# Decay rows fetched by one transfer per pair and sub-block, running products stored block by block, decays read back by one transfer per block

## The chip, the cores and the metric

The kernel runs on one core of a Trainium2 chip. The metric is the device time of one execution in microseconds. The kernel before takes 582.05 us, the median of three runs (582.04 to 582.39).

The core's engines are named as in the profile: PE (TensorE, matrix products), ACT (ScalarE), DVE (VectorE), POOL (GpSimd) and SP (SyncE, which here only issues DMA transfers). Each works through its own list in order; an instruction that has to wait holds up everything behind it on its engine.

## What is computed

A linear attention with decay, followed by two dense layers over 3072 tokens. With four sequences, eight heads, 768 positions, head dimension 32 and state size 16, the part of the reference that matters is:

```python
log_a = np.log(np.clip(a, 1e-06, 1.0))
for c in range(nc):                              # chunks; state is carried over
    cum = np.cumsum(la, axis=-1)
    L = np.exp(cum[:, :, :, None] - cum[:, :, None, :]) * causal
    M = np.einsum('bhin,bhjn->bhij', Cc, Bc) * L
    y = M @ xc + (Cc @ state) * np.exp(cum)
    state = exp(sum(la)) * state + sum_j(Bc_j xc_j exp(cum_last - cum_j))
h = y_tokens @ w_in                              # 3072x256 @ 256x2048
x = softplus(h) @ w_out                          # 2048 -> 256
h = x @ w2_in
out = piecewise(h) @ w2_out                      # 0, ((h+1)^2)/4 or h
```

The weights arrive as 64-bit floats; the kernel rebuilds 32-bit values from their bits.

## The kernel before

**Tiling.** The sequence is cut into NC = 6 blocks c of 128 positions, each with two sub-blocks s of 64. A unit u = 4c + b is one block of one sequence b, so there are 24 units; from block 1 on they are worked in pairs (u-1, u) with u odd. The dense layers are cut into steps s: `up` (first product of a 128-wide slice or two of the hidden dimension) and `down` (second product, summed in PSUM). Steps 0 to 95 belong to the first layer, 96 to 191 to the second.

**Attention.** In block 0 the decay matrix comes from logarithms (`log`, `spread` on PE, `decay` = exp on ACT). In the later blocks it is made of running products: `clip_load` loads all of `a`, `clip` (line 855) clips it, `store` (867) writes it to a DRAM tensor `clip_z`, and `rows` (903) reads a row of it back, broadcast to 64 partitions. `decay` (934) then turns the rows into the decay matrix by one DVE scan of 128x512. `runs` (872, 875) makes the running products within each sub-block by a scan, `store_runs` (881) writes them to a DRAM tensor `clip_p`, and `dec` (909) reads a block's share back, broadcast over the state index; `cd` (954) and the state update `carry_on` (1026) use it. Per unit, `scores` (C times B), `weigh` (line 987 on DVE, 989 on POOL: scores times decay), `sources`, then `st` and `out` on PE, `evac` (1090, 1092) and `ready` (1098) follow. Up to two units of block 0 have one of their two `weigh` steps on POOL (`WEIGH_POOL`, numbered 2u + half). The attention results and states of a unit use one PSUM area `y`, free again after `ready`.

**Weights.** Each of 8 pieces j of a weight matrix (kind i for the first product, o for the second) is loaded by SP (`load_w`, 668, 512 KB) into one of four staging buffers and rebuilt by `w0` (680 on DVE, 684 on ACT), `w1` (692), `w2` (704) and `w3` (716, which frees the staging buffer). `w_hi` (621 on ACT, 623 on DVE) and `split_w` (779) make a high and a low part. The same helper lines 621 and 623 serve the high part `g_hi` of the activations, and 1238 makes their low part `g_lo`. `g` (1223) is softplus on ACT; its table is loaded once (1222) before step 0.

**What sets the order.** `program()` lists all steps as jobs with a cost per engine, what they need, which buffers they take and give back, and a due time; `Jobs.order` then fills the engines' lists by a planner: it keeps a clock per engine, charges DVE and POOL extra where they overlap (`SHARED`), and among the steps that can begin first takes the one with the earliest due time. So a changed cost moves steps on every engine. Where PE has nothing to do early in the program the kernel puts in products of a zero tile (1342, `FILL`), as many as the planner's gap is long.

All DMA goes through SP. Eight semaphores are handed round, so a transfer cannot be issued before the one eight places ahead of it has landed.

Of the kernel before, what the change touches and what calls it, by code (L numbers as in the profile page):

```python
# [191 lines left out]
def pair_of(u):  # L192

    return u | 1
# [12 lines left out]
def program():  # L207
# [32 lines left out]
    add("clip_load", SP, 400, due=-1e5, takes=["t"], size=98e3)  # L240
# [3 lines left out]
    add("store_runs", SP, 1600, needs=["runs"], size=98e3, gives=["clip_load"])  # L244
    for c in range(1, NC):
        add(("dec", c), SP, 400 * DEC_DMAS, needs=["store_runs"], takes=["dec"], size=262e3)
    for u in range(NU):
# [4 lines left out]
        if c == 0:  # L252
            for hg in range(2):
                add(
                    ("spread", u, hg), PE, 470, needs=[("columns", hg), ("rows_of", u)] + ([("spread", u, 0)] if hg else []),
                    takes=[("acc", "h")] + [("ld", "lp")] * (hg == 0),
                )
                add(("decay", u, hg), ACT, 520, needs=[("spread", u, hg)], gives=[("part", ("spread", u, hg), 0)])
            decay = [("decay", u, 0), ("decay", u, 1)]
        else:  # L260
            add(("rows", u), SP, 800, needs=["store"] + [("rows", u - 1)] * (b % 2), takes=["lp"] * (b % 2 == 0), size=262e3)
            add(("decay", u), DVE, 1130, needs=[("rows", u)])
            decay = [("decay", u)]
            add(("cd", u), DVE, 200, needs=[("load", u), ("dec", c)])
# [8 lines left out]
        if b % 2:  # L273
            v = u // 2
            add(
                ("scores", v), PE, 640 if c else 1270, needs=[("load_bc", v)] + (decay + [("decay", u - 1)] if c else [("scores", v - 1)] * v),
                takes=["y", "acc", "acc"] if c else ["y"] + [("acc", "h")] * 2 if v == 0 else [("h", "acc")] * 4,
                gives=[("load_bc", v)],
            )
# [12 lines left out]
        if c == 0 or b % 2:  # L292

            needs = [("weigh", i, hg) for i in both for hg in range(2)] + ([("out", both[0] - 1)] if u else [])
            if c > 0:
                add(
                    ("st", u), PE, 850, needs=needs + [("sm", u - NB)], takes=["y"], gives=[("sources", i) for i in both],
                )
# [3 lines left out]
            add(  # L302
                ("out", u), PE, 750 if c else 750, needs=needs, takes=["y"] * (c == 0),
                gives=[("load", i) for i in both] + [("rows", u - 1) if c else ("part", ("spread", u, 0), 1)]
# [159 lines left out]
    DVE: {"w1": 1.1, "w2": 0.95, "w3": 0.95, "decay": 0.36, "split_w": 0.3, "g_lo": 1.1, "g": 0.8, "g_hi": 1.7, "t_lo": 1.1, "t_sum": 1.1, "s_sum": 1.1, "s_lo": 1.1, "clip": 0.3, "runs": 0.3},  # L464
# [3 lines left out]
WEIGH_POOL = [3, 6]  # L468
# [18 lines left out]
DEC_DMAS = 2  # L487
# [10 lines left out]
def tile_kernel(ctx: ExitStack, tc: tile.TileContext, a0, al, bc, ub, w_in, w_out, w2_in, w2_out, out):  # L498
# [117 lines left out]
    clip_p = dram.tile([NC * 2, H, NB, HALF], F32, name="clip_p")  # L616
# [230 lines left out]
    @job  # L847
    def clip_load(engine):
        tiles["clip"] = new(of("clip_load"), F32, "clip0").rearrange("p (h i) -> p h i", h=H)[0:nr]
        nc.sync.dma_start(tiles["clip"], al.rearrange("r (h i) -> r h i", h=H))  # L850
# [46 lines left out]
    @job  # L897
    def rows(engine, u):

        c, b = divmod(u, NB)  # L900
        r = b * NC + c
        for s in range(2):
            nc.sync.dma_start(flat(ld_t(u)[s * HALF:(s + 1) * HALF]), clip_z[r, s:s + 1].to_broadcast([HALF, H * HALF]))

    @job
    def dec(engine, c):
        for s in range(2):
            src = clip_p[2 * c + s].rearrange("h b i -> h (b i)")
            nc.sync.dma_start(
                dec_t(c)[:, s].rearrange("p b i -> p (b i)"), src.unsqueeze(1).to_broadcast([H, N, NB * HALF])  # L910
            )

    def dec_t(c):
        return flat(mine("dec", c)[0]).rearrange("p (s b i) -> p s b i", s=2, b=NB)

    def ld_t(u):
        if u >= NB:
            t = flat(buf(*got["rows", u & ~1][0])).rearrange("p (u h i) -> p u h i", u=2, h=H)
            return t[:, u % 2]
        return buf(*got["spread", u, 0][1])  # L920
# [29 lines left out]
    @job  # L950
    def cd(engine, u):

        t = parts(u)[2].rearrange("p (s i) -> p s i", s=2)
        nc.vector.tensor_tensor(out=t, in0=t, in1=dec_t(u // NB)[:, :, u % NB], op=ALU.mult)
# [66 lines left out]
    def carry_on(u, s):  # L1021

        c, b = divmod(u, NB)
        for i in range(2):
            state = s_t[b // 2][:, i]
            nc.vector.scalar_tensor_tensor(
                out=state, in0=state, scalar=dec_t(c)[:, s, b - 1 + i, HALF - 1:HALF], in1=states_t(u, s)[:, i],
                op0=ALU.mult, op1=ALU.add,
            )
# [366 lines left out]
```

## Time and profile before

| | before |
|---|---|
| median of three runs | 582.05 us (582.04 to 582.39) |
| the profiled execution | 585.17 us, of which the span is 583.4 us |
| PE busy in the span | 566.5 us (97%) |
| DVE / ACT / POOL busy | 443.9 / 337.6 / 38.2 us |
| mean granted TensorE clock | 0.992 |

The profile is of one execution. Its span runs from the first to the last instruction; 1.8 us of its time lie around it. It took 3.1 us more than the median run. Times in the rows are microseconds from the start of the span unless marked ns. The granted clock is a share of full speed (2.4 GHz); 0.50 means 1.2 GHz. A row of a timeline reads: start, duration, engine, line, operation, written tile <- read tiles, shapes, count, and in brackets the idle time of the engine before it and what ended it. The busy time of matmuls includes their pipelined ends, so the distance between starts is the better measure of their rate.

### The profile page before, as it was taken

What the parts mean: (1) busy time and instruction counts of PE and PEld (TensorE: products, weight loads), DVE (VectorE), ACT (ScalarE), POOL (GpSimd) and SP (SyncE); (2) the same over time, 40 slices, a digit from 0 to 9 for tenths busy, and PEclk for the clock granted to TensorE, in tenths of its full rate; (3) what the DMA queues carried; (4) which work ended last, traced back from release to release, by engine and by line L of the source; (5) the groups of instructions that cost most, each with busy time, mean ns of one, the idle gap of its engine ahead of it and who ended that gap; (6) DMA issues with size and microseconds to landing.
All of it is one profiled execution on the core that took longest, in us unless ns stands there. A gap on an engine that the chain in (4) does not pass through costs nothing.

```text
span 583.4 us, 10890 instructions
## 1 busy us (share of the span) xinstructions
PE 566.5 (97%) x4358; PEld 469.2 (80%) x4358; DVE 443.9 (76%) x812; ACT 337.6 (58%) x607; POOL 38.2 (7%) x40
## 2 busy tenths in 40 slices
PE   6898999999999999999999999999999999999997
PEld 3597999998787777788888788888887888788885
DVE  6795987755655774679999897987799767777674
ACT  5865543423323422466656687767677674777863
POOL 4210300000000320020000000200011000000000
PEclk9898999999999999999999999999999999999999
DMA  7957334413303200013332000000100000100001
GB/s 277 341 155 220 134 101 125 152 36 101 115 4 101 74 1 1 2 36 110 117 104 105 1 0 1 1 2 0 73 0 1 1 1 23 50 0 2 1 1 72
DMA packets 21062, 38.54 MB, mean 66 GB/s; under 512 B 2484, under 2 KB 4148, under 8 KB 21012
## 3 DMA queue, kind: packets, MB, share of 16 engines
q1 hardware_dynamic: 21012, 37.86, 19.6%
q8 instruction: 34, 0.56, 0.4%
q14 instruction: 16, 0.13, 0.1%
HBM read 34.50 MB, written 3.34 MB: 65 GB/s over the span
## 4 chain that ended last, share of the span: by engine, by line
PE 86%; DVE 7%; issue 3%; DMA 2%; ACT 1%; SPq 0%; DVEq 0%; ACTq 0%
PE acc L1264 42%; PE h L1128 6%; PE h L1129 5%; PE h L1130 5%; PE h L1135 3%; PE h L1137 3%; PE h L1136 3%; PE z L1135 3%; PE z L1137 3%; PE z L1136 3%; PE y L1038 2%; PE z L1130 1%; PE z L1128 1%; PE z L1129 1%; DMA st<-in_w_in_dram 1%
## 5 line engine op out<-in xcount | busy, mean ns | idle before, releaser
L1238 DVE TENSOR_TENSOR gl<-g,gh 128x512 fp32r<-128x512 f32 x184 | 127.9, 697 | 36.4 <-PE acc L1264 21.2
L1264 PE MATMUL acc<-gh,woh 128*128 128x512 f32 (+1 forms) x424 | 152.9, 368 | 0.2 <-DVE gh L623 0.2
L1264 PE MATMUL acc<-gh,wol 128*128 128x512 f32 (+1 forms) x424 | 150.7, 363 | 0.0
L1264 PE MATMUL acc<-gl,woh 128*128 128x512 f32 (+1 forms) x424 | 115.8, 364 | 1.1 <-DVE gl L1238 1.1
L1223 ACT ACTIVATE g<-h 128x512 f32<-128x512 f32 x74 | 44.1, 597 | 103.5 <-PE h L1130 103.0
L1264 PEld LDWEIGHTS acc<-gh,woh 128*128 128x128 f32 x424 | 80.0, 189 | 14.9 <-issue 0.9
L1264 PEld LDWEIGHTS acc<-gh,wol 128*128 128x128 f32 x424 | 80.0, 189 | 12.4
L1264 PEld LDWEIGHTS acc<-gl,woh 128*128 128x128 f32 x424 | 74.2, 189 | 14.7 <-DVE gl L1238 2.2
L621 ACT CAST gh<-g 128x512 fp32r<-128x512 f32 x98 | 60.8, 620 | 31.0 <-PE acc L1264 20.2
L1128 PE MATMUL h<-xh,wih 128*128 128x256 f32 (+1 forms) x224 | 76.4, 341 | 2.3 <-ACT g L1223 2.3
L623 DVE CAST gh<-g 128x512 fp32r<-128x512 f32 x88 | 40.1, 458 | 47.0 <-ACT g L1223 42.6
L1129 PE MATMUL h<-xh,wil 128*128 128x256 f32 (+1 forms) x224 | 74.2, 331 | 0.0
L1130 PE MATMUL h<-xl,wih 128*128 128x256 f32 (+1 forms) x224 | 74.1, 331 | 0.0
L1215 ACT ACTIVATE t<-t 128x512 f32<-128x512 f32 x96 | 60.8, 634 | 2.2
L1128 PEld LDWEIGHTS h<-xh,wih 128*128 128x128 f32 x224 | 43.0, 192 | 7.5 <-ACT g L1223 2.5
L1130 PEld LDWEIGHTS h<-xl,wih 128*128 128x128 f32 x224 | 43.1, 192 | 3.9
L1129 PEld LDWEIGHTS h<-xh,wil 128*128 128x128 f32 x224 | 43.1, 192 | 3.6
L1208 ACT ACTIVATE t<-h 128x512 f32<-128x512 f32 x37 | 22.1, 598 | 14.8 <-PE h L1137 11.5
L934 DVE TENSOR_TENSOR_SCAN ld<-ld,eye_t 128x512 f32<-128x512 f32 x20 | 25.5, 1274 | 2.6 <-DMA ld<-clip_z 2.5
L1208 ACT ACTIVATE t<-z 128x512 f32<-128x512 f32 x35 | 20.8, 595 | 9.8 <-PE z L1137 7.7
L1227 DVE TENSOR_TENSOR g<-h,t 128x512 f32<-128x512 f32 x37 | 25.4, 686 | 0.9 <-ACT t L1215 0.2
L1227 DVE TENSOR_TENSOR g<-z,t 128x512 f32<-128x512 f32 x35 | 23.9, 686 | 0.6
(339 smaller groups left out, 894.3 us busy)
## 6 DMA issues: line engine op xcount, KB each, us to landing
st<-in_w_in_dram SPq DMA_DIRECT2D x15, 512.0 KB, 6.6
st<-in_w_out_dram SPq DMA_DIRECT2D x15, 512.0 KB, 3.5
u<-in_ub_dram SPq DMA_DIRECT2D x24, 256.0 KB, 3.2
ld<-clip_z SPq DMA_DIRECT2D x40, 128.0 KB, 3.2
bc<-in_bc_dram SPq DMA_DIRECT2D x12, 384.0 KB, 8.1
out_dram<-st_plain SPq DMA_DIRECT2D x6, 256.0 KB, 2.3
dec<-clip_p SPq DMA_DIRECT2D x10, 128.0 KB
out_dram<-dec_plain SPq DMA_DIRECT2D x4, 256.0 KB, 2.9
```

The lines of the kernel that those rows point to most:

```text
L621: nc.scalar.copy(out, in_)
L623: engines[engine].tensor_copy(out, in_)
L1128: nc.tensor.matmul(o, wh, xh[c][:, k, t0:t0 + n], start=(k == 0), stop=False)
L1129: nc.tensor.matmul(o, wl, xh[c][:, k, t0:t0 + n], start=False, stop=False)
L1130: nc.tensor.matmul(o, wh, xl[c][:, k, t0:t0 + n], start=False, stop=(k == 1))
L1135: nc.tensor.matmul(bank, wh, bh, start=start, stop=False, skip_group_check=True)
L1208: nc.scalar.activation(out=t, in_=ph, func=act_funcs.IDENTITY_SAT240, scale=SAT)
L1215: nc.scalar.activation(out=t, in_=t, func=AF.Square, scale=0.5 / SAT, bias=0.5)
L1223: nc.scalar.activation(out=g, in_=ph, func=AF.Softplus)
L1227: nc.vector.tensor_tensor(out=g, in0=ph, in1=t, op=ALU.max)
L1238: engines[engine].tensor_tensor(out=mine("g_lo", s)[0], in0=mine("g", s)[0], in1=mine("g_hi", s)[0].bitcast(F32), op=ALU.subtract)
L1264: nc.tensor.matmul(acc_t(s, e), w, g[:, j * n:(j + 1) * n], start=(begins(e, j) and g is gh and i == 0), stop=(fc + j == NFC - 1 and g is ...
```

## The change

One unit's rows were read by two transfers (one per sub-block), four per pair; now a pair's rows come by two transfers (one per sub-block, both units in each), so twice the bytes in each, and both `decay` scans of a pair need both. The rows of `a` are ordered by block, sequence, sub-block instead of sequence, block, sub-block. The running products are stored by five transfers, one per block 1 to 5, instead of four, one per sequence; their tile is `more0` instead of one of the two buffers `t` that `w1` and `act_first` use. A block's decays come by one transfer (2 KB per partition) instead of two (1 KB each). In the planner the costs of `scores`, `st` and `out` on PE go up for the later blocks, `w0` on DVE is charged for overlap with POOL, and `WEIGH_POOL` names other steps. No step of the arithmetic is added or removed.

```diff
-    add("clip_load", SP, 400, due=-1e5, takes=["t"], size=98e3)
+    add("clip_load", SP, 400, due=-1e5, size=98e3)
-    add("store_runs", SP, 1600, needs=["runs"], size=98e3, gives=["clip_load"])
     for c in range(1, NC):
-        add(("dec", c), SP, 400 * DEC_DMAS, needs=["store_runs"], takes=["dec"], size=262e3)
+        add(("store_runs", c), SP, 600, needs=["runs"], size=16e3)
+        add(("dec", c), SP, 400, needs=[("store_runs", i) for i in range(1, NC if c == 2 else 2)], takes=["dec"], size=262e3)
...
-            add(("rows", u), SP, 800, needs=["store"] + [("rows", u - 1)] * (b % 2), takes=["lp"] * (b % 2 == 0), size=262e3)
-            add(("decay", u), DVE, 1130, needs=[("rows", u)])
+            if b % 2:
+                add(("rows", u), SP, 1100, needs=["store"], takes=["lp"], size=524e3)
+            add(("decay", u), DVE, 1130, needs=[("rows", pair_of(u))])
...
-                ("scores", v), PE, 640 if c else 1270, needs=...
+                ("scores", v), PE, 830 if c else 1270, needs=...
...
-                    ("st", u), PE, 850, needs=needs + [("sm", u - NB)], ...
+                    ("st", u), PE, 990, needs=needs + [("sm", u - NB)], ...
...
-                ("out", u), PE, 750 if c else 750, needs=needs, ...
+                ("out", u), PE, 1220 if c else 750, needs=needs, ...
...
-    DVE: {"w1": 1.1, "w2": 0.95, "w3": 0.95, "decay": 0.36, ...
+    DVE: {"w0": 1.1, "w1": 1.1, "w2": 0.95, "w3": 0.95, "decay": 0.36, ...
-WEIGH_POOL = [3, 6]
+WEIGH_POOL = [2, 5]
...
-    clip_p = dram.tile([NC * 2, H, NB, HALF], F32, name="clip_p")
+    clip_p = dram.tile([NC, H, NB * 2, HALF], F32, name="clip_p")
...
-    def store_runs(engine):
-        n = NC * 2
-        for b in range(NB):
-            nc.sync.dma_start(clip_p[:, :, b], tiles["clip"][b * n:(b + 1) * n])
+    def store_runs(engine, c):
+        n = NB * 2
+        nc.sync.dma_start(clip_p[c].rearrange("h r i -> r h i"), tiles["clip"][c * n:(c + 1) * n])
...
+        t = flat(buf(*got["rows", u][0])).rearrange("p (u f) -> p u f", u=2)
         for s in range(2):
-            nc.sync.dma_start(flat(ld_t(u)[s * HALF:(s + 1) * HALF]), clip_z[r, s:s + 1].to_broadcast([HALF, H * HALF]))
+            nc.sync.dma_start(
+                t[s * HALF:(s + 1) * HALF], clip_z[u - 1:u + 1, s].unsqueeze(0).to_broadcast([HALF, 2, H * HALF])
+            )
...
     def dec(engine, c):
-        for s in range(2):
-            src = clip_p[2 * c + s].rearrange("h b i -> h (b i)")
-            nc.sync.dma_start(
-                dec_t(c)[:, s].rearrange("p b i -> p (b i)"), src.unsqueeze(1).to_broadcast([H, N, NB * HALF])
-            )
+        src = clip_p[c].rearrange("h r i -> h (r i)")
+        nc.sync.dma_start(flat(mine("dec", c)[0]), src.unsqueeze(1).to_broadcast([H, N, NB * Q]))
```

**What moves.** Line numbers of the kernel after are one to three lower below line 881. First, on DVE, the start of block 0, from the clipping of `a` to the first piece of weights (`ld_117` and `ld_118` are the decay tiles of units 0 and 1, `w_257` or `w_256` the first weight piece). Before:

```order
L855 TENSOR_SCALAR dec_134<-clip_192 48x8x63
L680 TENSOR_SCALAR w_257<-st_135 128x512
L987 TENSOR_TENSOR ld_117<-y,ld_117 128x512
L987 TENSOR_TENSOR ld_118<-acc_215,ld_118 128x512
L987 TENSOR_TENSOR ld_117<-y,ld_117 128x512
L704 SCALAR_TENSOR_TENSOR w_257<-w_257,t 128x512
L716 SCALAR_TENSOR_TENSOR w_257<-st_135,w_257 128x512
L1098 TENSOR_TENSOR xl_307<-y,xh_306 128x2x128
```

Now:

```order
L855 TENSOR_SCALAR dec_134<-more_147 48x8x63
L680 TENSOR_SCALAR w_256<-st_135 128x512
L984 TENSOR_TENSOR ld_117<-y,ld_117 128x512 x2
L704 SCALAR_TENSOR_TENSOR w_256<-w_256,t 128x512
L716 SCALAR_TENSOR_TENSOR w_256<-st_135,w_256 128x512
L984 TENSOR_TENSOR ld_118<-acc_216,ld_118 128x512
L1095 TENSOR_TENSOR xl_303<-y,xh_302 128x2x128
```

Both `weigh` steps of unit 0 now stand together, and DVE's step of unit 1 follows two weight steps later; POOL has the other step of unit 1, now ahead of its last small product for that unit (`bt_258`) instead of behind it.

Second, on ACT, the steps ahead of the first softplus (`s_67` and `xh` are written by `evac`, `sm` by the state copy, `w_` tiles are weights). Before:

```order
L1107 ACTIVATE sm_140<-s_66,of_one 128x2x32 x2
L1090 CAST xh_306<-y 128x2x128
L1092 COPY s_67<-y 128x64
L692 ACTIVATE g<-raw,low_bias 128x512
L684 ACTIVATE w_396<-raw 128x512
L1222 ACT_TABLE_LOAD
L1223 ACTIVATE gh<-h_158 128x512
```

Now:

```order
L1104 ACTIVATE sm_140<-s_66,of_one 128x2x32 x2
L692 ACTIVATE g<-raw,low_bias 128x512
L1087 CAST xh_302<-y 128x2x128
L1089 COPY s_67<-y 128x64
L684 ACTIVATE w_349<-st_138 128x512
L1219 ACT_TABLE_LOAD
L1220 ACTIVATE gh<-h_158 128x512
```

One of the two weight steps between the evacuation of unit 2 and the table load has gone ahead of that evacuation.

Third, on SP, the stretch with the first rows and the running products (`st_` are the staging buffers of weights, `ld_120` and `ld_121` the tiles of rows). Before:

```order
L668 DMA st_138<-in_w_in_dram 128x2x512
L668 DMA st_135<-in_w_out_dram 128x2x512
L881 DMA clip_p<-clip_192 96x1x64 x4
L903 DMA ld_121<-clip_z 64x512 x2
L903 DMA ld_120<-clip_z 64x512 x2
L668 DMA st_136<-in_w_in_dram 128x2x512
L909 DMA dec_133<-clip_p 128x1x256 x2
L668 DMA st_137<-in_w_out_dram 128x2x512
L909 DMA dec_134<-clip_p 128x1x256 x2
```

Now:

```order
L901 DMA ld_121<-clip_z 64x2x512 x2
L901 DMA ld_120<-clip_z 64x2x512 x2
L668 DMA st_138<-in_w_in_dram 128x2x512
L880 DMA clip_p<-more_147 8x8x64 x5
L668 DMA st_135<-in_w_out_dram 128x2x512
L668 DMA st_136<-in_w_in_dram 128x2x512
L668 DMA st_137<-in_w_out_dram 128x2x512
L908 DMA dec_133<-clip_p 128x1x512
L908 DMA dec_134<-clip_p 128x1x512
```

The stores of running products stand one weight load earlier, the second pair of row transfers is gone from between the weight loads into `st_135` and `st_136`, and both `dec` transfers stand behind the load into `st_137`.

## Rows read from the trace of the kernel before

**Rows 1.** The page's first part: busy time of PE, share of the span.

```profile
PE 566.5 (97%) x4358; PEld 469.2 (80%) x4358; DVE 443.9 (76%) x812; ACT 337.6 (58%) x607; POOL 38.2 (7%) x40
```

**Rows 2.** Waits of PE: who waited for whom, total us, times, longest.

```profile
PE h L1128 <- ACT g L1223: 2.3, 1, 2.3
...
PE acc L1264 <- DVE gl L1238: 1.1, 2, 0.8
```

**Rows 3.** Windows: length, busy us per engine (instructions), granted clock, DMA share, GB/s.

```profile
14.00:16.00 2.00, 2.00 (x37) 1.76 (x40) 1.12 (x2) 1.15 (x3) 0.81 (x3) 0.67 1.05 388
16.00:18.00 2.00, 2.00 (x11) 0.31 (x7) 1.17 (x3) 1.15 (x3) 0.42 (x1) 0.50 1.04 390
...
20.00:30.00 10.00, 8.56 (x93) 6.95 (x93) 8.75 (x15) 8.84 (x19) 1.81 (x2) 1.00 0.90 309
...
52.00:54.00 2.00, 1.48 (x7) 1.48 (x8) 1.50 (x3) 1.51 (x3) 0.00 (x0) 0.56 0.75 247
54.00:56.00 2.00, 2.00 (x12) 2.00 (x12) 0.94 (x3) 1.53 (x3) 0.00 (x0) 0.59 0.74 258
```

**Rows 4.** Timeline of PE, the first 32 us.

```profile
13.45 0.59 PE L1342 MATMUL y<-idle 128*128 128x512 bf16 x2 [2.74 <-DVE ld L987]
...
19.94 1.67 PE L1342 MATMUL y<-idle 128*128 128x512 bf16 x7 [1.12 <-DVE xl L1098]
...
26.05 1.99 PE L1252 MATMUL acc<-gh,w 128*128 128x256 f32 x8 [1.44 <-DVE wil L779]
```

**Rows 5.** Timeline of ACT, the first 60 us.

```profile
23.40 0.69 ACT L684 ACTIVATE w<-raw 128x512 f32<-128x512 f32 x1
24.11 1.28 ACT L1222 ACT_TABLE_LOAD   x1
...
46.98 0.79 ACT L692 ACTIVATE t<-st,low_bias 128x512 uint32<-128x512 uint32 x1 [2.50 <-DMA dec<-clip_p]
...
51.23 0.75 ACT L692 ACTIVATE t<-st,low_bias 128x512 uint32<-128x512 uint32 x1 [2.64 <-DMA st<-in_w_out_dram]
51.88 0.58 ACT L1223 ACTIVATE g<-h 128x512 f32<-128x512 f32 x1
```

**Rows 6.** Timeline of SP's queue, 36 to 45 us.

```profile
36.52 3.34 SPq L881 DMA_DIRECT2D clip_p<-clip  x4
39.90 2.44 SPq L903 DMA_DIRECT2D ld<-clip_z  x4
42.45 0.52 SPq L668 DMA_DIRECT2D st<-in_w_in_dram  x1
...
44.48 0.41 SPq L668 DMA_DIRECT2D st<-in_w_out_dram  x1
```

**Rows 7.** Timeline of POOL, the products of units 0 and 1.

```profile
8.94 0.56 POOL L942 TENSOR_TENSOR bt<-u,ld 128x64 f32<-128x64 f32 x2 [0.38 <-DMA u<-in_ub_dram]
...
10.04 1.28 POOL L989 TENSOR_TENSOR ld<-g,ld 128x512 f32<-128x512 f32 x1
```

**Rows 8.** Timeline of DVE, the first 24 us.

```profile
10.18 1.43 DVE L680 TENSOR_SCALAR w<-st 128x512 f32<-128x512 f32 x1 [1.35 <-DMA st<-in_w_in_dram]
...
12.72 0.68 DVE L987 TENSOR_TENSOR ld<-y,ld 128x512 f32<-128x512 f32 x1
```

**Rows 9.** Timeline of DVE, the scan of the running products.

```profile
35.27 1.22 DVE L875 TENSOR_TENSOR_SCAN clip<-dec,dec 48x512 f32<-48x512 f32 x1
```

**Rows 10.** Timeline of all engines from 198 us: POOL's sums beside DVE's scan.

```profile
199.12 1.29 POOL L743 TENSOR_TENSOR dec_plain<-xh,xl 128x512 f32<-128x512 f32 x1 [130.40 <-DVE s L1026]
...
201.87 2.31 DVE L934 TENSOR_TENSOR_SCAN ld<-ld,eye_t 128x512 f32<-128x512 f32 x1
```

**Rows 11.** The page: the scan's group (busy us, mean ns, idle before) and DMA issues (KB, us to landing).

```profile
L934 DVE TENSOR_TENSOR_SCAN ld<-ld,eye_t 128x512 f32<-128x512 f32 x20 | 25.5, 1274 | 2.6 <-DMA ld<-clip_z 2.5
...
u<-in_ub_dram SPq DMA_DIRECT2D x24, 256.0 KB, 3.2
ld<-clip_z SPq DMA_DIRECT2D x40, 128.0 KB, 3.2
```

More of the change, by code (lines that the diff above doesn't have):

```diff
@@ L275, in program @@
             add(
-                ("scores", v), PE, 640 if c else 1270, needs=[("load_bc", v)] + (decay + [("decay", u - 1)] if c else [("scores", v - 1)] * v),
+                ("scores", v), PE, 830 if c else 1270, needs=[("load_bc", v)] + (decay + [("decay", u - 1)] if c else [("scores", v - 1)] * v),
                 takes=["y", "acc", "acc"] if c else ["y"] + [("acc", "h")] * 2 if v == 0 else [("h", "acc")] * 4,
@@ L296, in program @@
                 add(
-                    ("st", u), PE, 850, needs=needs + [("sm", u - NB)], takes=["y"], gives=[("sources", i) for i in both],
+                    ("st", u), PE, 990, needs=needs + [("sm", u - NB)], takes=["y"], gives=[("sources", i) for i in both],
                 )
@@ L302, in program @@
             add(
-                ("out", u), PE, 750 if c else 750, needs=needs, takes=["y"] * (c == 0),
-                gives=[("load", i) for i in both] + [("rows", u - 1) if c else ("part", ("spread", u, 0), 1)]
+                ("out", u), PE, 1220 if c else 750, needs=needs, takes=["y"] * (c == 0),
+                gives=[("load", i) for i in both] + [("rows", u) if c else ("part", ("spread", u, 0), 1)]
                 + [("sources", u, 0)] * (c == 0),
@@ L463 @@
 SHARED = {
-    DVE: {"w1": 1.1, "w2": 0.95, "w3": 0.95, "decay": 0.36, "split_w": 0.3, "g_lo": 1.1, "g": 0.8, "g_hi": 1.7, "t_lo": 1.1, "t_sum": 1.1, "s_sum": 1.1, "s_lo": 1.1, "clip": 0.3, "runs": 0.3},
+    DVE: {"w0": 1.1, "w1": 1.1, "w2": 0.95, "w3": 0.95, "decay": 0.36, "split_w": 0.3, "g_lo": 1.1, "g": 0.8, "g_hi": 1.7, "t_lo": 1.1, "t_sum": 1.1, "s_sum": 1.1, "s_lo": 1.1, "clip": 0.3, "runs": 0.3},
     POOL: {"t_sum": 0.3, "t_lo": 0.3, "t_hi": 0.3, "s_sum": 0.3, "s_lo": 0.3, "g_lo": 0.25, "weigh": 0.4, "sources": 1.0, "cd": 1.1, "sm": 0.6, "split_w": 0.4},
@@ L848, in clip_load @@
     def clip_load(engine):
-        tiles["clip"] = new(of("clip_load"), F32, "clip0").rearrange("p (h i) -> p h i", h=H)[0:nr]
+        tiles["clip"] = more[0].rearrange("p (h i) -> p h i", h=H)[0:nr]
         nc.sync.dma_start(tiles["clip"], al.rearrange("r (h i) -> r h i", h=H))
@@ L898, in rows @@
     def rows(engine, u):
[L900 to L901 removed]
+        t = flat(buf(*got["rows", u][0])).rearrange("p (u f) -> p u f", u=2)
         for s in range(2):
[L903 removed]
+            nc.sync.dma_start(
+                t[s * HALF:(s + 1) * HALF], clip_z[u - 1:u + 1, s].unsqueeze(0).to_broadcast([HALF, 2, H * HALF])
+            )
     @job
     def dec(engine, c):
[L907 to L911 removed]
+        src = clip_p[c].rearrange("h r i -> h (r i)")
+        nc.sync.dma_start(flat(mine("dec", c)[0]), src.unsqueeze(1).to_broadcast([H, N, NB * Q]))
     def dec_t(c):
[L914 removed]
+        return mine("dec", c)[0]
     def ld_t(u):
         if u >= NB:
[L918 removed]
+            t = flat(buf(*got["rows", pair_of(u)][0])).rearrange("p (u h i) -> p u h i", u=2, h=H)
             return t[:, u % 2]
@@ L951, in cd @@
     def cd(engine, u):
-        t = parts(u)[2].rearrange("p (s i) -> p s i", s=2)
-        nc.vector.tensor_tensor(out=t, in0=t, in1=dec_t(u // NB)[:, :, u % NB], op=ALU.mult)
+        t = parts(u)[2]
+        nc.vector.tensor_tensor(out=t, in0=t, in1=dec_t(u // NB)[:, u % NB], op=ALU.mult)
     def cb_t(u, hg):
@@ L1026, in carry_on @@
             nc.vector.scalar_tensor_tensor(
-                out=state, in0=state, scalar=dec_t(c)[:, s, b - 1 + i, HALF - 1:HALF], in1=states_t(u, s)[:, i],
+                out=state, in0=state, scalar=dec_t(c)[:, b - 1 + i, (s + 1) * HALF - 1:(s + 1) * HALF], in1=states_t(u, s)[:, i],
                 op0=ALU.mult, op1=ALU.add,
@@ L1362 @@
     c6 = C.reshape(NB, H, NC, Q, N)
[L1363 removed]
+    al = np.ascontiguousarray(a.reshape(NB, H, NC, 2, HALF).transpose(2, 0, 3, 1, 4)).reshape(NC * NB * 2, H * HALF)
     a0 = np.ascontiguousarray(a6[:, :, 0]).reshape(NB * H, Q)
```

2 lines of the change are left out of this document (removed).

## The prediction, made before the change was run

> **What bounds the kernel now.** I read the page's first part first: PE is busy for 566.5 of 583.4 us, 97% [rows 1]. So only three things can pay: PE's idle stretches, some 17 us in all, the stretches in which its granted clock is low, and work on PE itself, which the change does not touch. DVE, ACT, POOL and the transfers matter only where PE waits for them. Next I read PE's timeline, its waits and the windows, to find where the idle time lies, and then the other engines' timelines there.
>
> There are three such places. The first is the start. PE stands idle for 2.74 us ahead of 13.45, where its zero-tile products and `out` of unit 0 wait for the last `weigh` of DVE; for 1.12 us ahead of 19.94; and for 1.44 us ahead of the first `down` at 26.05 [rows 4]. Over the four microseconds behind the first gap the granted clock is 0.67 and 0.50, while from 20 to 30 us, behind both the smaller gaps, it is 1.00 [rows 3]. So a long gap is paid for twice, a short one once.
>
> The second place is at 50 us. PE waits once for 2.3 us for ACT's softplus [rows 2], and behind it the clock is 0.56 and 0.59 over 52 to 56 us [rows 3]. The softplus itself takes 0.58 at 51.88, but it stands behind a weight step (`w1`, 51.23) that had waited 2.64 us for a load; the `w1` at 46.98 had waited 2.50 [rows 5]. SP's queue tells why those loads were late: at 36.52 it spends 3.34 us on issuing the four stores of running products and at 39.90 2.44 on four row transfers, and only then, at 42.45 and 44.48, the two weight loads [rows 6].
>
> The third is at about 204 us, layer 1's end: two waits of 1.1 us together for `g_lo` of DVE [rows 2]. DVE is late there because of POOL's sums: a scan of 128x512, 1.27 us on average [rows 11], takes 2.31 there [rows 10].
>
> **The change, part by part.** The sum goes against the profiled execution, 585.17 us, 3.1 more than the median run.
>
> *A, the start.* POOL's `weigh` now stands ahead of the small product that began behind 9.50 (8.94 + 0.56), so it begins at 9.50 and not at 10.04 [rows 7]. DVE's `w0` at 10.18 lasts 1.43 [rows 8] where ACT's takes 0.69 [rows 5], and it ends at 11.61, just behind POOL's end at 11.32 [rows 7]: it waits for POOL, and so ends 0.54 sooner. Then only two `weigh` steps instead of three stand ahead of `out` of unit 0, each 0.60 from start to start (0.68 busy) [rows 8]. The gap of 2.74 becomes 2.74 - 0.54 - 0.60 = 1.60. That is near the 1.12 and 1.44 after which the clock stayed up, and far from 2.74, so I take the clock as staying up: 2 x 0.33 + 2 x 0.50 = 1.66 us regained [rows 3]. Against this the kernel has three more zero-tile products ahead of `out` of unit 1, 1.67 / 7 = 0.24 each [rows 4], 0.72. Net: 0.54 + 0.60 + 1.66 - 0.72 = 2.08. Ahead of the first softplus ACT has one `w0` of 0.69 fewer behind its last evacuation [rows 5], so that the table load at 24.11 comes 2.08 + 0.69 = 2.77 sooner. The first `down` also needs the low part of the weights from DVE [rows 4], whose list is hardly shorter, so I take 2.6: **-2.6**. Lower end of the gain: if the clock falls as before, 2.77 - 1.66 = 1.1. Upper end: 2.8.
>
> *B, the wait at 50 us.* The stores now stand one weight load earlier, the rows of the second pair have moved ahead of them, and both `dec` transfers stand behind the loads. So nothing is queued between the moment a staging buffer comes free and its load; the loads go out some 6 us sooner, of the 3.34 + 2.44 [rows 6], against waits of 2.5 and 2.64 [rows 5]. The wait of 2.3 [rows 2] goes: **-2.3**. What is late next is ACT's own work: if one weight step and the softplus, 0.75 + 0.58 [rows 5], are then still behind, only -1.0 is left, the lower end.
>
> *C, the clock behind it.* 2 x 0.44 + 2 x 0.41 = 1.70 of lost time at 52 to 56; PE is busy for only 1.48 of the first two microseconds [rows 3], so I take off 0.2: **-1.5**. It falls with B.
>
> *D, a new wait at about 35 us.* The scan of the running products, 1.22 [rows 9], stood behind the low part of weight piece 2 on DVE and now stands ahead of it and of piece 3's, and beside POOL's own two weight steps. Nothing of before shows this place, so I bound it: 0 if the pieces are early enough, 1.22 if they are not, and 1.22 + 2.31 - 1.27 = 2.26 if POOL blocks the scan as in [rows 10]. A gain is excluded, since nothing is taken from this place. I take about the middle: **+1.0**.
>
> *E, the end of layer 1.* Two scans of the last pair now stand in a row ahead of one `g_lo`, while POOL's sums (1.29 each [rows 10]) run; before, one did. The waits of 1.1 [rows 2] could vanish if POOL's sums fall elsewhere (-1.1), or grow by a whole second stretched scan (+2.3). One stretched scan made 1.1; a second that overlaps the sums only in part I put at half of that: **+0.5**.
>
> *F, the rest.* Per pair, two row transfers of 256 KB replace four of 128 KB. Each scan of a pair needs both, so a pair's first scan may begin later by the other unit's 256 KB, 1.06 us at the 247 GB/s of [rows 3]. DVE waited 2.5 us in all for rows, over 20 scans, and a transfer of 256 KB (`u`) landed 3.2 us from issue as one of 128 KB did [rows 11]. The rows' tile is asked for a pair ahead. I take nothing; the bounds are 0 and 1.06 per pair.
>
> The Trainium skill ("DMA: Bandwidth & Descriptors", section "Anatomy of one DMA — SWDGE (gpsimd) path") speaks against this: a fixed 2.0 us and the bytes at 436 GB/s on top, a fit for transfers that GpSimd issues. By that an estimate is 2.3 us for 128 KB and 2.6 for 256 KB, 0.3 later for each of ten pairs, and 3 us if none were covered, which would make the sum 580.2. The equal 3.2 of [rows 11] does not show it.
>
> Sum: -2.6 - 2.3 - 1.5 + 1.0 + 0.5 = -4.9, so the profiled execution goes from 585.17 to 580.3, and the median of 582.05 to **577.2**.
>
> **The rivals.** *The first clock fall stays.* A gap of 1.60 lies between 1.44, which cost no clock, and 2.74, which did; nothing here shows the point between. Then A loses 1.66: 578.8. *The gap at layer 1's end grows and pulls the clock down:* E at +2.3 and 1.0 of slow clock behind it, less than C since the gap came in two parts: 577.2 + 1.8 + 1.0 = 580.0, from a gap near 2.3 us on. *It does not do what it says:* the loads come sooner, but the weight steps on DVE and ACT are themselves late, so that PE waits as long, and D eats A: 582. For it speaks that DVE is busy for 443.9 us; against it, that ACT idled 2.50 and 2.64 there, for transfers alone [rows 5]. *The pairs wait a little:* 0.3 of F's 1.06 are not covered, ten times: 580.2. *Slower:* each pair's first scan waits for the whole 512 KB of rows. DVE runs late, `scores` and `out` with it, and PE waits at each of ten pairs. With nothing covered that is 577.2 + 10.6 = 587.8; it makes the kernel slower from 0.6 us per pair on. Against both: DVE waits for rows only 2.5 in all today [rows 11], although the rows come in the same queue as the weights.
>
> **How the numbers follow.** Chances: forecast 0.57, first clock fall 0.18, end of layer 1 0.08, pairs waiting a little 0.04, no gain 0.08, slower 0.05. A measurement of this kernel can tell about 0.2% from no change, 1.2 us, which is 580.9 to 583.2. The first four cases lie below it: faster 0.87, same 0.08, slower 0.05. The range reaches down to 574.6 (D at 0 and E at -1.1, that is 1.0 + 1.6 less) and up to 580.3, over the clock's, the layer end's and the small pair wait's cases; the last two lie outside, 0.13.
>
> **What would show it.** A: a gap of about 1.6 ahead of `out` of unit 0, the clock 1.00 from 12 to 18 us, the first `down` at about 23.5. B and C: both loads issued by 39 us, no wait of PE for softplus at 48 to 52, no clock below 0.9 there. D: about 1 us of PE idle at 33 to 37. E: a gap of about 1.6 at layer 1's end. F: DVE's wait for rows near 2.5 in all. Wrong would be above all: a clock that falls at the start, a wait at 50 us that has a new releaser, or one wait per pair.

## The result, and the profile of the kernel after

The kernel after takes 576.28 us, the median of four runs (575.48 to 576.46), against 582.1 for the kernel before in the same session. The ratio is 0.9896, with a 95% interval of 0.9879 to 0.9913: 5.8 us or 1.0% faster. Forecast were 577.2 us, 4.9 less than before, so sign and size came out; the terms of the sum did not all, as the sections below show. One of the six runs of `shared_back` (below), 622.9 us at a mean clock of 0.852, is in a slower state and left out of its median.

The profiled execution of the kernel after took 576.36 us, with a span of 574.5. That is near its median, whereas the profiled execution of before (585.17) lay 3.1 above its own. So the two profiles differ by 8.8 us and the medians by 5.8, and it has to be shown which 3 us are not the change's.

The rows of after follow that answer to [rows 1 to 8], [rows 10] and [rows 11]. First the page's first part (busy time, share of the span):

```profile
PE 563.4 (98%) x4363; PEld 466.9 (81%) x4363; DVE 441.8 (77%) x813; ACT 334.7 (58%) x603; POOL 42.3 (7%) x43
```

Then windows (columns as in [rows 3]: length, busy time per engine, granted clock, DMA share, GB/s):

```profile
14.00:16.00 2.00, 1.74 (x29) 0.98 (x28) 1.92 (x3) 2.00 (x5) 1.28 (x1) 1.00 1.05 387
16.00:18.00 2.00, 0.86 (x5) 0.39 (x5) 1.80 (x4) 2.00 (x7) 0.00 (x0) 1.00 1.05 389
...
52.00:54.00 2.00, 2.00 (x19) 2.00 (x18) 2.00 (x5) 2.00 (x4) 0.00 (x0) 1.00 0.07 28
54.00:56.00 2.00, 2.00 (x19) 2.00 (x19) 2.00 (x4) 1.97 (x5) 0.00 (x0) 1.00 0.00 0
```

PE's timeline, with the waits at 34, at 50 and at the end of layer 1; it answers to [rows 2] and [rows 4]:

```profile
11.23 0.59 PE L1339 MATMUL y<-idle 128*128 128x512 bf16 x2 [0.39 <-DVE ld L984]
...
17.14 1.45 PE L1339 MATMUL y<-idle 128*128 128x512 bf16 x6 [1.40 <-DVE xl L1095]
...
22.38 1.99 PE L1249 MATMUL acc<-gh,w 128*128 128x256 f32 x8
...
33.76 3.72 PE L1249 MATMUL acc<-gh,w 128*128 128x256 f32 x16 [0.20 <-ACT gh L1220]
...
50.72 0.39 PE L1125 MATMUL h<-xh,wih 128*128 128x256 f32 x1 [0.64 <-ACT g L1220]
...
203.71 0.74 PE L1261 MATMUL acc<-gl,woh 128*128 128x512 f32 x2 [0.57 <-DVE gl L1235]
```

ACT, the table load and the late weight step with the softplus behind it ([rows 5]):

```profile
20.43 1.28 ACT L1219 ACT_TABLE_LOAD   x1
...
49.44 0.75 ACT L692 ACTIVATE t<-st,low_bias 128x512 uint32<-128x512 uint32 x1 [2.69 <-DMA st<-in_w_in_dram]
50.09 0.58 ACT L1220 ACTIVATE g<-h 128x512 f32<-128x512 f32 x1
```

SP's queue ([rows 6]), the stores of running products and what now follows them:

```profile
27.34 6.50 SPq L880 DMA_DIRECT2D clip_p<-more  x5
34.88 0.40 SPq L668 DMA_DIRECT2D st<-in_w_out_dram  x1
36.02 0.39 SPq L668 DMA_DIRECT2D st<-in_w_in_dram  x1
37.07 0.37 SPq L668 DMA_DIRECT2D st<-in_w_out_dram  x1
37.49 1.29 SPq L908 DMA_DIRECT2D dec<-clip_p  x2
```

POOL's timeline of after, its first `weigh` ([rows 7]):

```profile
9.57 1.55 POOL L986 TENSOR_TENSOR ld<-g,ld 128x512 f32<-128x512 f32 x1
```

DVE's timeline of after: the first `w0` ([rows 8]), the scan of the running products ([rows 9]) and the last pair's two scans beside POOL's sums ([rows 10]):

```profile
9.55 0.43 DVE L680 TENSOR_SCALAR w<-st 128x512 f32<-128x512 f32 x1 [0.79 <-DMA st<-in_w_in_dram]
...
24.58 1.22 DVE L875 TENSOR_TENSOR_SCAN more<-dec,dec 48x512 f32<-48x512 f32 x1
...
197.54 4.48 DVE L931 TENSOR_TENSOR_SCAN ld<-ld,eye_t 128x512 f32<-128x512 f32 x2
```

And the page's groups of the scan and of the transfers of rows ([rows 11]):

```profile
L931 DVE TENSOR_TENSOR_SCAN ld<-ld,eye_t 128x512 f32<-128x512 f32 x20 | 25.9, 1319 | 1.0 <-DMA ld<-clip_z 0.9
...
ld<-clip_z SPq DMA_DIRECT2D x20, 256.0 KB, 3.9
```

What to see: PE's gap at the start is 0.39 where it was 2.74; the first `down` begins at 22.38 and not at 26.05; the clock is 1.00 in both places where it had fallen. PE still waits at 50 us, but 0.64 instead of 2.26, and the weight step behind which ACT waits 2.69 is that of a later load (piece 7's, issued at 41.53, as the order has it), since the two loads that were late before are now issued at 36.02 and 37.07.

### The profile page after: what moved, and what is told of

The parts are those of the page before. It is cut to its first block, busy times and chain, and to the rows that moved or that the text cites. A ratio compares the mean times of both kernels' runs of the same rounds, so it can differ in the third digit from the quotient of the medians.

```text
span 574.5 us, 10830 instructions
## 1 busy us (share of the span) xinstructions
PE 563.4 (98%) x4363; PEld 466.9 (81%) x4363; DVE 441.8 (77%) x813; ACT 334.7 (58%) x603; POOL 42.3 (7%) x43
## 4 chain that ended last, share of the span: by engine, by line
PE 88%; DVE 4%; DMA 4%; issue 1%; SPq 1%; ACT 1%; DVEq 0%; ACTq 0%
PE acc L1261 43%; PE h L1125 6%; PE h L1126 6%; PE h L1127 6%; PE h L1132 3%; PE h L1134 3%; PE h L1133 3%; PE z L1132 3%; PE z L1134 3%; PE z L1133 3%; DMA st<-in_w_in_dram 3%; DMA st<-in_w_out_dram 1%; PE y L1035 1%; PE z L1127 1%; PE z L1126 1%; PE z L1125 1%
## 5 line engine op out<-in xcount | busy, mean ns | idle before, releaser
L1235 DVE TENSOR_TENSOR gl<-g,gh 128x512 fp32r<-128x512 f32 x185 | 130.8, 709 | 34.4 <-PE acc L1261 21.2
L623 DVE CAST gh<-g 128x512 fp32r<-128x512 f32 x95 | 43.3, 459 | 57.1 <-ACT g L1220 52.6
L621 ACT CAST gh<-g 128x512 fp32r<-128x512 f32 x91 | 56.4, 620 | 30.8 <-PE acc L1261 20.6
```

Source lines behind the costliest of these rows:

```text
L621: nc.scalar.copy(out, in_)
L623: engines[engine].tensor_copy(out, in_)
L1235: engines[engine].tensor_tensor(out=mine("g_lo", s)[0], in0=mine("g", s)[0], in1=mine("g_hi", s)[0].bitcast(F32), op=ALU.subtract)
```

## The experiments

Each kernel was timed beside runs of the kernel before on the same chip in the same session; since before's median moved between sessions (582.08, 582.9 and 583.03), kernels of different sessions are compared by their ratio to it.

**The kernel before once more.** No edit.

> The kernel before, unchanged, profiled a second time. Theory 1: the profiled execution of before was an unusual one: its first weight load landed at 10.18 us, after POOL's weigh of 1.28 us had begun at 10.04, so DVE's w0 lost 1 us behind it and the long gap pulled the clock down; in the kernel after the same load landed at 9.55, just ahead of POOL's weigh at 9.57. Then an ordinary execution of before shows w0 at about 0.43, a gap ahead of out of unit 0 near 1.2 to 1.8, clock 1.00 over 12 to 18 us, the first down near 23.5 to 24.5 and a span of about 580.3; of the predicted 2.6 at the start only about 1 to 1.5 is in the median. Theory 2: the start is the same in all executions (gap near 2.7, clock 0.67 and 0.50), and the 3.1 us by which the profiled run was above the median lie elsewhere. Time: 582.1 by both.

Measured: 582.42 us, ratio 0.998 (0.996 to 1.000); the profiled execution had a span of 581.6. The start on its DVE timeline:

```profile
10.16 0.43 DVE L680 TENSOR_SCALAR w<-st 128x512 f32<-128x512 f32 x1 [1.41 <-DMA st<-in_w_in_dram]
```

On its POOL timeline:

```profile
10.28 1.43 POOL L989 TENSOR_TENSOR ld<-g,ld 128x512 f32<-128x512 f32 x1
```

On its PE timeline:

```profile
12.43 0.59 PE L1342 MATMUL y<-idle 128*128 128x512 bf16 x2 [1.48 <-DVE ld L987]
...
24.10 1.99 PE L1252 MATMUL acc<-gh,w 128*128 128x256 f32 x8 [1.46 <-DVE wil L779]
```

And two of its windows (the clock is the third number from the end):

```profile
14.00:16.00 2.00, 1.99 (x36) 1.11 (x32) 1.55 (x4) 2.00 (x6) 1.04 (x4) 1.00 1.05 388
...
52.00:54.00 2.00, 2.00 (x11) 2.00 (x11) 0.98 (x3) 1.38 (x3) 0.00 (x0) 0.50 0.64 168
```

Theory 1 holds in its main point: the same program, its load landing at the same 10.16 to 10.18, but here POOL's `weigh` began 0.12 later than DVE's `w0` and not 0.14 earlier. So `w0` took 0.43, the gap 1.48, the clock stayed up, and the first `down` came at 24.10 instead of 26.05. The start is a race, and the profile that the prediction was made from shows a lost one. One half of the theory fell: I had put the landing down to the kernel (9.5 after, 10.2 before). In later profiles it is 9.69 in a kernel with the old transfers (`early_runs`), and 9.29 (`tsum_dve`) to 10.13 (`bc_late`) with the new. Whether it changes with the execution or with the build isn't shown: the two kernels that were profiled twice have 10.18 and 10.16, 9.55 and 9.57. Between the two profiles of before it was POOL's start that moved.

The falls of the clock vary too. Of 55 runs of before in the three sessions, 31 have a mean granted clock of 0.998 or more and a median of 582.20, and 24 a lower one and a median of 583.63. Of nine runs of after one has 0.997; it took 579.2, the others 575.28 to 576.46. A mean does not tell where in a run the clock fell. The profiles do: in both of before and in the one of after at 0.997 it fell behind the wait at 50 us. With a fall at the start as well, the profile in front of the prediction has 0.992; five of the 55 have 0.993 or less.

**Transfers alone, planner's numbers alone, and one number alone.** From after, with the numbers of before (`dma_only`); from before, with the numbers of after (`numbers_only`); from before, `weigh_only`:

```
 dma_only:      scores 640, st 850, out 750; SHARED without "w0"; WEIGH_POOL = [3, 6]
 numbers_only:  scores 830, st 990, out 1220; SHARED with "w0": 1.1; WEIGH_POOL = [2, 5]
 weigh_only:    WEIGH_POOL = [2, 5]
```

> The kernel after with the planner's numbers of before (PE costs 640, 850, 750, no overlap charge for w0, WEIGH_POOL 3 and 6): only the transfers and the tile of the running products are changed. The start is then as in before. Theory of the queue: the rows of the second pair and both dec transfers no longer stand ahead of the two weight loads, only the stores do (about 3.4 us), so the two loads go out some 2.4 and 3 us sooner; PE's wait for softplus at 50 us shrinks from 2.3 to under 0.7 and no clock falls there: -3 us, 579. Rival: the weight steps on DVE and ACT bind there anyway, so the wait stays near 2: 581 to 582.

> The kernel before with the planner's numbers of after (PE costs, overlap charge for w0, WEIGH_POOL 2 and 5), its transfers as they were. The start is then as in after (first down near 22.4). In SP's list the stores of running products come before a weight load, but rows, and one dec of two transfers, still stand around the two late loads. Theory of the queue: about 2.4 us of rows ahead of the first of them and 1.3 of dec ahead of the second leave a wait near 1 to 1.5 at 50 us: 579. Rival: the order alone does it all, 576.3.

> The kernel before with only WEIGH_POOL changed to 2 and 5. By the planner, POOL's weigh then comes third, and the two late weight loads stand in a row ahead of both dec transfers, but behind the stores and the rows. Theory: the start gains 1 to 1.5 in the median and the wait at 50 us stays at 1.5 to 2 with its fall of the clock: 580.5. Rival (the start is worth the predicted 2.6 also in the median): 579.5.

Measured: `dma_only` 578.77, ratio 0.9919 (0.9892 to 0.9945); `numbers_only` 578.53, 0.9916 (0.9895 to 0.9936); `weigh_only` 583.81, 1.0002 (0.9987 to 1.0018). SP's queue in `dma_only`:

```profile
33.89 3.42 SPq L880 DMA_DIRECT2D clip_p<-more  x5
37.78 0.40 SPq L668 DMA_DIRECT2D st<-in_w_in_dram  x1
38.74 0.40 SPq L668 DMA_DIRECT2D st<-in_w_out_dram  x1
```

PE's wait for softplus there, from the waits (total us, times, longest):

```profile
PE h L1125 <- ACT g L1220: 1.1, 1, 1.1
```

SP's queue of `numbers_only`, where PE has no wait at 50 us at all:

```profile
27.26 4.95 SPq L881 DMA_DIRECT2D clip_p<-clip  x4
...
35.70 0.52 SPq L668 DMA_DIRECT2D st<-in_w_in_dram  x1
...
37.70 0.40 SPq L668 DMA_DIRECT2D st<-in_w_out_dram  x1
```

And PE's wait in `weigh_only`, whose stores are at 34.48 and whose two loads go out at 40.41 and 41.05:

```profile
PE h L1128 <- ACT g L1223: 1.9, 1, 1.9
```

Each half gives some 4.5 us against before and both together some 6; by the rows both shorten the same wait. My expectation for `numbers_only` was too high: rows and `dec` transfers still stand between its loads, and PE does not wait there. The stores go out at 27.26 instead of 34.57 (`before_same`). `weigh_only` gained nothing, though its first `down` is at 23.96, so its theory (580.5) and its rival (579.5) both failed; its wait at 50 us, the clock that falls behind it and two more waits for weights of 0.8 and 0.6 stand against it.

**The stores earlier, nothing else.** From before:

```diff
-    add("runs", DVE, 1500, needs=...)
+    add("runs", DVE, 1500, due=24000, needs=...)
```

> The kernel before with one edit: the scan of the running products has an earlier due time, so that the planner puts it and the four stores of running products some 6 us earlier, ahead of one more weight load; the transfers, the tiles, WEIGH_POOL and the costs are those of before, and so is the start up to 20 us. Theory of the queue, as corrected by the first runs (the stores are what made the two weight loads late, not the rows and the dec transfers): the two loads are issued near 35 and 38 us instead of 40.5 and 42.5, PE's wait of 2.3 us for softplus at 50 us goes, and no clock falls there: 2 to 3 us less than before in the median. Rival: the planner's other reordering or the start made the difference, and it stays within 1 us of before.

Measured: 579.4 us, ratio 0.9948 (0.9935 to 0.9962), with before at 582.08. SP's queue:

```profile
27.98 4.53 SPq L881 DMA_DIRECT2D clip_p<-clip  x4
...
34.80 0.37 SPq L668 DMA_DIRECT2D st<-in_w_in_dram  x1
...
39.05 0.39 SPq L668 DMA_DIRECT2D st<-in_w_out_dram  x1
```

PE's wait for softplus at 50 us is gone and no clock falls there: 2.7 us, with the transfers, tiles, `WEIGH_POOL` and costs of before. This is the cleanest run of the study: one due time, and steps B and C are seen nearly by themselves. Part of the 2.7 may be the start (its first `down` is at 23.61, against 24.10 in `before_same`); the planner also moved a few weight steps.

**After once more, and a pair's rows by four transfers or by one.** `after_same` is unchanged. In `rows_by_unit` only the issue in `rows` differs; in `rows_one` the rows of `a` are ordered by block, pair, sub-block, unit, so that one transfer can fill the tile. Of both edits only the new issue in `rows` is shown:

```diff
 # rows_by_unit
+        for i in range(2):
+            for s in range(2):
+                nc.sync.dma_start(t[s * HALF:(s + 1) * HALF, i],
+                                  clip_z[u - 1 + i, s:s + 1].to_broadcast([HALF, H * HALF]))
 # rows_one
+        nc.sync.dma_start(flat(...), clip_z[u // 2].unsqueeze(1).to_broadcast([2, HALF, 2 * H * HALF]))
```

> The kernel after, unchanged, on the chip of the next three runs, as their yardstick and for a second look at its start. Theory of the race: its first weight load again lands near 9.5 us (in the two kernels with the changed transfers it did so, at 9.50 and 9.55; in four profiles with the old transfers at 10.04 to 10.25), w0 on DVE takes 0.43 and PE's gap ahead of out of unit 0 is near 0.4. Rival: the landing varies from execution to execution and is near 10.1 here, with w0 near 1.3 and a gap of 1.2 to 1.6. Time 576.3; no fall of the clock before the end.

> The kernel after with one edit: a pair's rows come by four transfers of 128 KB (one per unit and sub-block) instead of two of 256 KB; planner, order and bytes are unchanged. Theory of PE's waits: a product that reads rows by more than one transfer needs more semaphores than one instruction waits for, so PE gets separate wait instructions in its stream; before has 31 of them ahead of the products of x and the weighed scores, after has 11, and the first 32 of these products of a pair take 0.38 instead of 0.27 us from start to start. Then this kernel has 31 again and is slower by 20 x 0.055 = 1.1 us than after. Rival 1: the waits are hidden and the two kernels are the same within 0.2. Rival 2, the first-scan wait of the prediction: each scan needs only its own unit's rows again, so it is faster by up to 1 us.

> The kernel after with a pair's rows by a single transfer of 512 KB over all 128 partitions (the rows of a are ordered by block, pair, sub-block, unit for that; the decay tile is read with that order); planner and order are unchanged. Theory of PE's waits: one more wait instruction per pair goes from PE's stream, 10 x 0.05 = 0.5 us less than after. Rival: a pair's first scan, or a weight load behind the larger transfer, is later, and the time is as after or up to 1 us more.

Measured, before at 582.08: `after_same` 575.98 us, ratio 0.9893 (0.9878 to 0.9909); `rows_by_unit` 577.08, 0.9907 (0.9892 to 0.9922); `rows_one` 644.42, 1.105 (1.102 to 1.108). The race of `after_same` came out as I had expected (load at 9.57, `w0` 0.44, no gap to speak of), but its profiled execution is the one of 579.2 us: PE waited 2.16 at 50 us and the clock fell behind it.

Why `rows_by_unit` is slower is seen at the line of the products of `x` and the weighed scores. One row of the view of that line counts separate wait instructions in PE's stream (count; shortest, median and longest in ns; first and last start). In before:

```profile
L1038 PEldq EVENT_SEMAPHORE  x31: 51/51/1384, 22.0 to 237.3; - x31
```

In after:

```profile
L1035 PEldq EVENT_SEMAPHORE  x11: 51/51/51, 13.6 to 224.4; - x11
```

In `rows_by_unit`:

```profile
L1036 PEldq EVENT_SEMAPHORE  x31: 51/51/51, 14.7 to 228.3; - x31
```

And the first 32 such products of one pair, with those of the next kind behind them, on PE's timeline of after:

```profile
140.44 0.45 PE L1035 MATMUL y<-ld,u 64*32 64x64 f32 x32
140.71 0.59 PE L1013 MATMUL y<-u,bt 64*32 64x64 f32 x32
```

The same pair in `rows_by_unit`:

```profile
140.64 0.54 PE L1036 MATMUL y<-ld,u 64*32 64x64 f32 x25
...
141.03 0.57 PE L1014 MATMUL y<-u,bt 64*32 64x64 f32 x30
```

From the first product to the bulk of the next kind it is 0.27 us in after and 0.39 with four transfers. Summed from the records' starts over all ten pairs these products take 7.64 us in before, 7.57 in `numbers_only`, 7.73 in `rows_by_unit`, and 6.50 in after and 6.52 in `dma_only`. So the transfers' number costs PE 1.1 us, 20 waits of 0.055. It costs nothing on DVE, whose wait for rows is 0.0 in `rows_by_unit` and 0.9 in after: rival 2 is right about DVE, but PE does not gain by it. That a product which reads rows from more transfers has more semaphores to wait for, and that the surplus becomes instructions, is the reading of these counts. The Trainium skill ("Perfetto Trace Analysis", section "Identifying Dependency Chains") comes near it: an instruction that waits for several engines may get EventSemaphore instructions ahead of it; here it is several transfers, at 51 ns each. By the time alone the 1.1 us between the two kernels is not beyond the intervals; the rows carry it.

`rows_one` shows two things. The page's group of the scan:

```profile
L929 DVE TENSOR_TENSOR_SCAN ld<-ld,eye_t 128x512 f32<-128x512 f32 x20 | 23.8, 1214 | 57.4 <-DMA ld<-clip_z 57.4
```

And two of its windows, while one such transfer runs:

```profile
112.00:114.00 2.00, 2.00 (x19) 2.00 (x18) 0.00 (x0) 0.00 (x0) 0.00 (x0) 1.00 0.13 51
114.00:116.00 2.00, 0.29 (x3) 0.09 (x1) 0.00 (x0) 0.00 (x0) 0.00 (x0) 1.00 0.13 50
```

The expected gain isn't there (the wait instructions stay at 11, so what the last one of each pair waits for is open), and the rival came, far larger than I had put it: DVE waits 57.4 us for rows instead of 0.9, and the kernel, at a mean clock of 0.955, loses 62 us against before. The transfer moves 50 GB/s at a DMA share of 0.13, which is 2 of 16 engines. The Trainium skill has the rule ("DMA: Bandwidth & Descriptors", section "Rules for kernel authors"): an outermost dimension smaller than 16, such as a leading broadcast, keeps a transfer on at most that many engines. The outermost dimension here is 2, in after's transfers 64; the trace agrees.

**What is left in after.** `shared_back` drops the planner's overlap charge of `w0`; `bc_late` moves one transfer in SP's list; `tsum_dve` sets `T_POOL = 0`, so that DVE makes the sums at the end of layer 1; `bc_late_tsum` has both of these:

```diff
 # shared_back
-    DVE: {"w0": 1.1, "w1": 1.1, ...
+    DVE: {"w1": 1.1, ...
 # bc_late, behind the planner
+    names = [r[0] for r in result]
+    late = result.pop(names.index(("load_bc", 5)))
+    result.insert([r[0] for r in result].index(("load_w", 0, "o", 7)) + 1, late)
```

> The kernel after without the planner's overlap charge for w0 on DVE. By the planner's order the running products are then scanned and stored some 6 us later again, ahead of the two late weight loads, as in before; transfers, WEIGH_POOL and PE costs are those of after. Theory: the charge is what moved the stores, and the stores are what made PE wait at 50 us: a wait of 1 to 1.5 us there, as in the run with the changed transfers alone (1.1), so 1 to 2 us more than after: 577 to 578. Rival: the stores in eight-partition pieces cost the queue less, and it stays at 576.3.

> The kernel after with one transfer moved in SP's list alone: the load of B and C for pair 5 (384 KB), which stands ahead of three late weight loads though its scores come much later, now stands behind them. What is left at 50 us in after is a wait of 0.6 us (2.2 with a fall of the clock in a second profile) for a weight load that takes 7.9 us to land. Theory of the shared path: between 35 and 49 us the transfers, not their issue, bind (DMA share 0.92), so 384 KB less ahead of that load bring it 1.3 us sooner at 300 GB/s: no wait at 50 us, no fall there, 0.6 to 1 us less than after, near 575.3 or 0.988 of before. Rival: the load is late because its staging buffer comes free late; then nothing changes.

> The kernel after with POOL's sums at the end of layer 1 made on DVE instead. Theory of the prediction's step E: DVE's two scans there take 4.48 us instead of 2.5 because POOL holds them up, and the g_lo behind them makes PE wait 0.57 us; without POOL's sums that wait goes and the time falls by 0.5 to 0.6. Rival: DVE's own sums (about 0.7 us each, eight operations) take the place of the stall and PE waits as long or longer a little later: 0 to 1 us more.

> Both of the foregoing edits in the kernel after. They lie 150 us apart; if both theories hold the gains add up to 1.1 to 1.6 us: near 574.7, 0.987 of before, the fastest of all kernels here. If one of them fails, it shows as its own single run.

Measured, before at 583.03: `shared_back` 577.23 us, ratio 0.9896 (0.9871 to 0.9922); `bc_late` 576.12, 0.9875 (0.9852 to 0.9898); `tsum_dve` 575.46, 0.9863 (0.9839 to 0.9887); `bc_late_tsum` 575.68, 0.9865 (0.9842 to 0.9888). The stores on SP's queue in `shared_back`:

```profile
34.08 1.71 SPq L880 DMA_DIRECT2D clip_p<-more  x5
```

Two of PE's waits there:

```profile
PE acc L1261 <- DVE wol L779: 0.8, 1, 0.8
PE acc L1261 <- DVE woh L623: 0.6, 1, 0.6
```

Its stores stand late again, yet PE doesn't wait for softplus at 50 us, and the ratio is that of after: my theory that their place alone decides fell with this run, and the rival came. The row of the five stores is 1.71 long there, against 6.50 in after, 3.42 in `dma_only` and, for four stores, 3.34 in before. The view by line tells issuing from waiting (count; shortest, median and longest issue in ns; first and last start). In before:

```profile
L881 SPq DMA_DIRECT2D clip_p<-clip x4: 758/776/882, 36.5 to 39.1; - x4
```

In after:

```profile
L880 SPq DMA_DIRECT2D clip_p<-more x5: 265/265/318, 27.3 to 33.6; - x5
```

And the longest of SP's own waits between the stores of after:

```profile
SPq L880 <- DMA st<-in_w_in_dram: 2.6, 1, 2.6
```

So a store by block takes SP about 0.3 us, one by sequence 0.77: five against four are 1.4 against 3.1 us. The other 5.0 us of after's row are waits for the landing of a weight load, of `u` and of two row transfers (2.6, 0.6 and 1.8), each of them eight places ahead in SP's list. In `shared_back` SP waits for no landing there, so its loads go out at 36.51 and 37.20 although the stores stand right ahead of them. The place of the stores and their cheaper issue are two ways to the same end. PE waits elsewhere instead, for weights, as in `weigh_only`.

`bc_late` removes the wait, but not as I had it: the load of piece 7 landed for ACT at 49.40, against 49.44 in after. Its start had lost the race (first `down` at 23.16), so PE came to the place 0.8 later and found nothing to wait for. So its ratio, the expected 0.988, does not speak for the theory. Whether the gain of a won race is given back there as a rule isn't shown: `tsum_dve` won it (first `down` at 22.10) and has no wait either, its piece 7 being there at 47.98. Over the six profiles whose order is after's in this stretch, but for the one moved load, ACT begins on piece 7 between 47.78 (`rows_by_unit`) and 50.98 (`after_same`), and PE waits in two. That the transfers' rate binds isn't shown.

`tsum_dve` did in its rows what was expected. The last pair's scans on its DVE timeline:

```profile
195.04 2.34 DVE L931 TENSOR_TENSOR_SCAN ld<-ld,eye_t 128x512 f32<-128x512 f32 x2 [0.44 <-DMA ld<-clip_z]
```

2.34 us instead of 4.48, and PE's wait for `g_lo` of 0.57 is gone. It is the lowest of all kernels, 0.3% below after by the ratios, but the intervals overlap, so that it beats after isn't settled. The two edits together gave no more than this one.

## Why the prediction came out, step by step

*A, the start (-2.6): direction right, the clock's term mis-sized.* In the profiles 3.67 us, 26.05 to 22.38. The predicted gap of 1.60 exists: it is 1.54 or 1.55 in the seven profiles of kernels with the new `WEIGH_POOL` in which POOL's `weigh` began before DVE's `w0`, and the clock didn't fall behind it. In the other three, after's among them, DVE began first (by 0.02 us in after) and the gap was 0.39 or less. What I took for a property of the kernel before, `w0` at 1.43 and the fall of the clock worth 1.66, was a lost race in one of two profiled executions. Against the second profile of before (24.10) the start gains 0.9 to 1.7, with the race lost or won in after. So the term that was mis-sized is the clock's: 1.66 in the profile, and little in the median, since few runs of before have a mean clock as low as that profile's. No run shows the start's share of the 5.8 us by itself.

*B, the wait at 50 us (-2.3): right in cause, most of the size.* The loads go out at 36.02 and 37.07 as forecast, and the wait fell from 2.26 to 0.64 (2.16 in one execution of after); what is left is for another load, piece 7's. I had named rows, `dec` and stores alike as what stands ahead; by `numbers_only`, `early_runs` and `shared_back` it is the 3.34 us of the stores.

*C, the clock behind it (-1.5): right in the profile, too large in the median.* 24 of 55 runs of before and one of nine of after have a lower mean clock; between the two groups of before lie 1.4 us. If all of these falls are the one at 50 us, it is worth some 0.6 in an average run (24/55 x 1.4, an estimate).

*D, the new wait at 35 us (+1.0): wrong.* PE waits 0.20 there, and for ACT. The scan of the running products ran at 24.58, 10.7 us earlier than before, and took 1.22, unstretched; POOL's weight steps hit a `w0` and a `w2` of DVE instead, which took 1.51 and 1.75, and PE had the pieces in time. I had placed the scan by the times of before, though the start was to come sooner and the scan had moved up in DVE's list.

*E, the end of layer 1 (+0.5): wrong in sign.* The scans in a row take 4.48 beside POOL's sums, as I feared, but they make one wait of 0.57 where before had two of 0.77 and 0.37. That comes with the transfers: `dma_only` has the one wait (0.56), `numbers_only` and `early_runs` have the two. `tsum_dve` confirms that POOL's sums are the cause of the wait that is left.

*F, the rows (0): wrong, and the one that I hadn't seen.* I had written that the change does not touch work on PE itself. A transfer of 256 KB lands 3.9 us from issue, 0.7 later than one of 128 KB, and PE didn't notice: DVE's wait for rows is 0.9 in after and 2.5 in before, and goes up and down between kernels without the time following (0.6 to 3.4 in the others with two transfers, 0.0 to 5.6 with four). The gain is on PE, 1.1 us of wait instructions. The row that could have told it (31 wait instructions at one line) was in the trace of before. How the rival in which pairs wait would look, `rows_one` shows, though there the transfer's rate makes it.

Between the two profiles these terms make 3.67 + 1.62 + 1.5 + 0.57 + 1.1 = 8.5 of the 8.8 us. For the median an estimate, with 0.9 to 1.7 for A, 0.6 for C and the profiles' figures for the rest, is 4.8 to 5.6 of 5.8. So the forecast's 4.9 came near by luck, with errors that offset each other: A's and C's clock terms hold 3.2 us, most of which only the profiled execution of before had, and D, E and F were together 3.2 too pessimistic (1.0 + 1.1 + 1.1). The 3.1 us by which that execution lay above its median was in the text, and I didn't ask which stretch had them.

## What to carry to other kernels

When the profiled execution lies well above the median, find what in it is chance before summing: two engines whose starts lie within 0.2 us of each other, as here, are a race, and a fall of the clock that the profile shows may be absent in most runs. Before a row of issues is called slow, look at what the queue itself waits for. Count the wait instructions of the bounding engine at each line; fewer, larger transfers can pay there even where no engine waits for data. And look at the outermost dimension of a transfer before merging two into one.

## What the runs showed of the hardware

DVE's `w0` took 0.43 to 0.49 when it began ahead of POOL's step, and 0.77 to 1.53 in the profiles where it began behind it; once POOL was itself the second, it took 1.43 (`before_same`) to 1.55 (after) instead of 1.27 to 1.29.

Separate wait instructions on PE cost 51 ns by their rows, and 0.055 us each in the distance of products.

A 512 KB broadcast whose outermost dimension is 2 moved 50 GB/s at a DMA share of 0.13, while after's transfers of rows, with 64, had part in 303 GB/s at a share of 0.99 in the two microseconds from 96 us, together with those of `u` and of B and C.

SP took 0.26 to 0.32 us to issue a store of running products by block and 0.76 to 0.88 for one by sequence.
